# First products of two expert layers by seven block products instead of eight, in a fused attention and two-expert kernel

## The chip, the cores and the metric

One core of a Trainium2 chip runs the whole program. The metric is device time in microseconds. Times are read from one profiled execution (its span runs from the first to the last instruction on the engines) and from three runs without a profile. TensorE (PE) multiplies, and its weight loads (PEld) are listed apart; VectorE (DVE), ScalarE (ACT) and GpSimd (Pool) do the rest, and SyncE (SP) issues the transfers.

## What is computed

Attention with hashed buckets on 16 heads (2 x 8) of 768 tokens, then a gated expert, then a second expert, on 1536 tokens of 512 features:

```
def _moe_ref(x, w_gate, w_val, w_out, rms_g) -> np.ndarray:
    rms = np.sqrt(np.mean(x * x, axis=-1, keepdims=True) + 1e-06)
    xn = x / rms * rms_g
    g = xn @ w_gate
    silu = g * (1.0 / (1.0 + np.exp(-g)))
    val = xn @ w_val
    return (silu * val @ w_out).astype(np.float32)
...
def _moe2_ref(x, w_in, w_out) -> np.ndarray:
    h = x @ w_in
    alpha = 1.0
    g = np.where(h > 0.0, h, alpha * (np.exp(np.minimum(h, 0.0)) - 1.0))
    return (g @ w_out).astype(np.float32)
```

The first expert has 1536 hidden features (12 tiles of 128), the second 2048 (16 tiles). The weights come in as 64-bit floats.

## The kernel before, in words

Every number that enters a matmul is kept as a high and a low word (two reduced-precision floats that add up to it), and each product is made in three passes (`PASS`, L948 and on): high by high, high by low, low by high. ACT makes the high word by a copy, DVE or Pool the low word by a subtraction.

*Attention* comes first: eight pairs of heads, with scores (`ps_s`, L557), transposes (`ps_p`, L602) and weighted sums (`ps_v`, L649). Its output, scaled and split, is `xn`: for each of two batches of 768 tokens, four depth tiles of 128 features.

*Expert one* goes through its 12 hidden tiles in groups of 3, 3, 2, 2, 2 (`SIZES`), and each group through blocks of tokens: four of 384 in the first group, three of 512 after (`BW`; the middle block straddles the two batches, so Pool copies it together, `mid`, L1003). `hidden` makes, for one tile and one block, the gate and value products (`proj_mm`, L993: 4 depth tiles x 3 passes each), then silu on ACT (L1036), the product of both on DVE (L1042), and the high and low words of the result (ACT L1057, DVE L1061) into one of four `pt` buffers. `reduce1` (L1079) multiplies a group's tiles by `w_out` into PSUM (`ps_y`, L1096) and adds the result to the running sum `ya` on DVE (L1108). After the last group `ya` is split into `y` (L1113, L1117).

*Expert two* goes the same way in groups of 3, 3, 3, 3, 2, 2 with 512 tokens a block; its nonlinearity takes exp on ACT and two DVE operations (L1045, L1051). `reduce_cols` (L1137) writes `ps_o` (L1151), with tokens on the rows, and DVE adds it to `oa` (L1163).

*Weights* of the next group are loaded by SP and turned from 64-bit to 32-bit floats: ACT takes the magnitude of the upper half (L891), Pool clamps it (L894), DVE shifts and joins bits in three steps (L900, L907, L914), and then ACT and Pool make high and low words (L936, L940).

PSUM has four single banks (`bank`: `ps_h` and the attention's) and two double ones (`bank2`: `ps_s`, `ps_y`, `ps_o`); each queue runs in the order in which the program issues it. That order is one written list, `ORDER`, of all planned tasks: `Plan.add` collects tasks with their reads and writes, and `Plan.run` issues them as the list says.

## Time and profile before

| | us |
|---|---|
| median of three runs | 808.13 (805.48 to 808.89) |
| the profiled execution's own time | 808.29 |
| its span | 806.5 |
| PE busy in the span | 793.1 |
| DVE busy | 576.0 |
| ACT busy | 414.8 |
| Pool busy | 347.4 |

The granted clock of PE has a mean of 0.998 of full speed (2.4 GHz). The matmuls of neighbouring rows overlap, so a mean duration is longer than the distance from one start to the next; the distance is read from the chain of waits, where rows follow one another.

### The profile page before, as it was taken

How to read it: one execution, taken by the hardware profiler on the slowest of the kernel's cores; microseconds unless marked ns; L12 is line 12 of the kernel's file. 1: busy time of each engine (PE TensorE's matmuls, PEld its weight loads, DVE VectorE, ACT ScalarE, POOL GpSimd, SP SyncE). 2: the span in 40 equal slices, each digit the busy share in tenths (PEclk: the TensorE clock that was granted, in tenths of full speed). 3: DMA queues.
4: the chain of work that ended last, by engine and by line, in shares of the span. 5: the costliest groups of instructions: out<-in, count | busy, mean ns of one | idle time of the engine just before them, and what ended most of it. 6: DMA issues, size and time to landing. Idle time of an engine off the chain costs nothing.

```text
span 806.5 us, 11405 instructions
## 1 busy us (share of the span) xinstructions
PE 793.1 (98%) x4282; PEld 690.9 (86%) x4282; DVE 576.0 (71%) x864; ACT 414.8 (51%) x776; POOL 347.4 (43%) x317
## 2 busy tenths in 40 slices
PE   8999999989999999999999999999999999999998
PEld 6999899878989998888888888888888888888786
DVE  7899999998986835525455567588656686784776
ACT  7999999988985733412222232354433243323230
POOL 5898889987887214212221233221231042221300
PEclk9999999999999999999999999999999999999999
DMA  5537653261021013104002222223203210112004
GB/s 193 183 110 256 227 150 108 98 187 30 1 79 41 1 41 130 53 1 130 3 26 78 79 66 67 77 79 118 78 1 118 60 46 27 52 28 78 0 1 157
DMA packets 28695, 65.64 MB, mean 81 GB/s; under 512 B 3040, under 2 KB 3424, under 8 KB 28640
## 3 DMA queue, kind: packets, MB, share of 16 engines
q1 hardware_dynamic: 28640, 64.91, 25.3%
q8 instruction: 34, 0.56, 0.3%
q14 instruction: 21, 0.17, 0.1%
HBM read 56.25 MB, written 3.15 MB: 74 GB/s over the span
## 4 chain that ended last, share of the span: by engine, by line
PE 82%; DVE 11%; ACT 2%; issue 2%; POOL 1%; DMA 1%; ACTq 0%; SPq 0%; DVEq 0%; POOLq 0%
PE ps_h L993 38%; PE ps_o L1151 16%; PE ps_y L1096 12%; PE ps_v L649 5%; PE ps_p L602 5%; PE ps_s L557 4%; DVE nm L564 3%; DVE pt L614 2%; DVE wf L907 1%; DVE h L1061 1%; ACT p L574 1%; ACT pt L610 1%; DVE wf L914 1%; PE ps_c L484 1%; DVE wf L900 1%
## 5 line engine op out<-in xcount | busy, mean ns | idle before, releaser
L940 POOL TENSOR_TENSOR wlo<-wf,whi 128x768 fp32r<-128x768 f32 (+1 forms) x54 | 90.7, 1687 | 187.8 <-ACT whi L936 171.7
L993 PE MATMUL ps_h<-xn,whi 128*128 128x512 f32 (+1 forms) x480 | 138.3, 369 | 0.0
L894 POOL TENSOR_SCALAR wf<-wf 128x768 f32<-128x768 f32 (+1 forms) x54 | 45.5, 848 | 198.7 <-ACT wf L891 198.2
L1151 PE MATMUL ps_o<-whi,h 128*128 128x512 f32 (+1 forms) x388 | 118.9, 387 | 0.5 <-DVE h L1061 0.4
L993 PE MATMUL ps_h<-y,whi 128*128 128x512 f32 x384 | 118.2, 389 | 0.0
L1057 ACT CAST h<-hf 128x512 fp32r<-128x512 f32 (+1 forms) x87 | 52.0, 605 | 125.1 <-DVE hf L1042 66.0
L993 PEld LDWEIGHTS ps_h<-xn,whi 128*128 128x128 f32 x480 | 88.4, 188 | 11.7
L649 PE MATMUL ps_v<-pt,vv 128*128 128x256 f32 x576 | 94.9, 293 | 2.2 <-DVE ot L667 2.2
L1036 ACT ACTIVATE sg<-ps_h 128x512 f32<-128x512 f32 (+1 forms) x87 | 49.9, 580 | 91.4 <-PE ps_h L993 59.5
L1061 DVE TENSOR_TENSOR h<-hf,h 128x512 fp32r<-128x512 f32 (+1 forms) x87 | 68.7, 806 | 34.9 <-ACT h L1057 34.7
L564 DVE TENSOR_REDUCE nm<-ps_s 128x1 f32<-128x768 f32 x96 | 90.6, 946 | 3.0 <-PE ps_s L557 2.2
L574 ACT ACTIVATE p<-ps_s,nm 128x768 f32<-128x768 f32 x96 | 87.4, 911 | 8.1 <-DVE nm L564 6.8
L1096 PE MATMUL ps_y<-h,whi 128*128 128x512 f32 (+1 forms) x312 | 91.2, 373 | 0.3 <-DVE h L1061 0.3
L557 PE MATMUL ps_s<-tk,tq 128*128 128x384 f32 x384 | 87.9, 350 | 1.5 <-ACT p L574 1.0
L993 PE MATMUL ps_h<-xn,wlo 128*128 128x512 f32 (+1 forms) x240 | 88.2, 367 | 0.0
L614 DVE TENSOR_TENSOR pt<-ps_p,pt 128x512 fp32r<-128x512 f32 x120 | 80.6, 682 | 10.5 <-ACT pt L610 9.7
L1151 PEld LDWEIGHTS ps_o<-whi,h 128*128 128x128 f32 x388 | 72.6, 188 | 16.2 <-DVE h L1061 0.8
L993 PEld LDWEIGHTS ps_h<-y,whi 128*128 128x128 f32 x384 | 72.1, 188 | 14.9
L649 PEld LDWEIGHTS ps_v<-pt,vv 128*128 128x128 f32 x576 | 80.0, 190 | 5.6 <-DVE ot L667 2.5
L602 PE MATMUL ps_p<-ident,p 128*128 128x128 f32 x576 | 82.5, 276 | 1.9 <-DVE pt L614 0.8
L1151 PE MATMUL ps_o<-wlo,h 128*128 128x512 f32 (+1 forms) x194 | 75.1, 387 | 0.0
L993 PE MATMUL ps_h<-y,wlo 128*128 128x512 f32 x192 | 74.7, 389 | 0.0
(102 smaller groups left out, 1419.7 us busy)
## 6 DMA issues: line engine op xcount, KB each, us to landing
wraw<-in_moe_w_out_dram SPq DMA_DIRECT2D x12, 768.0 KB, 4.6
qk<-in_heads_dram SPq DMA_DIRECT2D x16, 384.0 KB, 5.2
wraw<-in_moe_w_in_dram SPq DMA_DIRECT2D x8, 768.0 KB, 4.5
qq<-in_heads_dram SPq DMA_DIRECT2D x14, 384.0 KB, 5.3
kk<-in_heads_dram SPq DMA_DIRECT2D x14, 384.0 KB, 5.6
wraw<-in_moe_w_out_dram SPq DMA_DIRECT2D x10, 512.0 KB, 4.1
tq<-tq SPq DMA_DIRECT2D x21, 192.0 KB, 3.3
vn<-in_v_dram SPq DMA_DIRECT2D x8, 384.0 KB, 5.8
```

What stands on the lines that cost most here:

```text
L557: nc.tensor.matmul(st[B_][:, hf, 0:HS], lhsT=tq[:, x, c * 128:(c + 1) * 128], rhs=tk[:, x, hf * HS:(hf + 1) * HS], start=(x == 0), stop=(x ...
L564: nc.vector.tensor_reduce(out=st["nm", u, cc], in_=st[B_][:, :, 0:HS], axis=AX.XY, op=ALU.max, negate=True,)
L574: nc.scalar.activation(out=halves(st["p", u][:, cc]), in_=st.pop(B_)[:, :, 0:HS], func=AF.Exp, bias=st["nm", u, cc], scale=1.0, accum_out= ...
L602: nc.tensor.transpose(out=st[B_][:, o:o + 128], in_=p[:, cc, (2 * n + kt) * 128:(2 * n + kt + 1) * 128], identity=ident,)
L614: nc.vector.tensor_tensor(out=pt[:, 1], in0=st.pop(B_), in1=f(pt[:, 0]), op=ALU.subtract)
L649: nc.tensor.matmul(st[B_][:, 0:256], lhsT=st["vv", j][:, a, 2 * n + kt, :], rhs=pt[:, x, kt * 256:(kt + 1) * 256], start=(n == seq[0] and ...
L940: nc.gpsimd.tensor_tensor(out=l, in0=s["w"], in1=f(h), op=ALU.subtract)
L993: nc.tensor.matmul(ps[:, o:o + ln], lhsT=w[wp][:, kk, ft * 128:(ft + 1) * 128], rhs=t[xp][:, s:s + ln], start=(kk == 0 and n == 0), stop=( ...
L1057: nc.scalar.copy(out=st["h", g, blk, ft][:, 0, 0:bw], in_=s["hf"])
L1061: nc.vector.tensor_tensor(out=h[:, 1, 0:bw], in0=s["hf"], in1=f(h[:, 0, 0:bw]), op=ALU.subtract)
L1096: nc.tensor.matmul(s["ps"][:, 0:bw], lhsT=wo[wp][:, ft, m * 128:(m + 1) * 128], rhs=h[:, xp, 0:bw], start=(ft == 0 and i == 0), stop=(ft = ...
L1151: nc.tensor.matmul(s["ps"], lhsT=h[:, xp, t * 128:(t + 1) * 128], rhs=wo[wp][:, ft, ds], start=(ft == 0 and i == 0), stop=(ft == n - 1 and ...
```

## The change

The first products of both experts are made of blocks. The two batches (768 tokens each) are the two block rows, the two halves of the depth (256 features each) the inner blocks, and two hidden tiles the two block columns. A pair of block columns then has eight block products; the new code makes seven, of sums of blocks, and adds them up (Strassen's scheme). In expert one a pair is the gate and the value of one hidden tile, and nine of twelve tiles go this way; in expert two a pair is two hidden tiles, and seven pairs (14 of 16 tiles) do. The first three tiles of expert one and the first two of expert two (`G2`) are still made directly, in blocks of 384 tokens. In the new source the lines of the old operations have moved: L993 is L1065, L1096 is L1158, L1108 is L1170, L1151 is L1218, L1163 is L1231.

- `pair(q, j)`: the seven products for one pair and one half (384 tokens) of each batch, 6 matmuls each (L1518), in three PSUM banks. Bank `ps_wA` collects products 1, 6, 7 and 4 one after the other and is read after each: copies by ACT (L1536), then additions by DVE (L1539); `ps_wC` collects 5 and 3, `ps_wE` holds 2. The two (expert one, L1586, L1596) or four (expert two, L1558, L1569) hidden tiles come out as high and low words as before. The second DVE step of the old nonlinearity of expert two becomes a Relu on ACT (L1555).
- `pair_weights`: loads and converts one pair's weights at a time, in pieces of 512 columns (L1372 to L1391), makes four sums of weight blocks on Pool (L1442) and seven split operands (ACT L1452, Pool L1456).
- `spread_x` and `spread_t`: form and split the four sums of token blocks of each expert, for both depth tiles (DVE and Pool, L1314, L1327; L1258, L1269). Two of the four go to Pool (`TPOOL`).
- `reduce1` takes one hidden tile a time in the nine pairs, so a group has three matmuls, and DVE adds to `ya` nine times more, not four; in `reduce_cols` a group is always two tiles.
- The copies for the middle block go, and `ORDER` is a new list for the whole program, attention included. In attention the operations are the same, but for two Pool operations of the first pair that are cut in halves.

```diff
-SIZES = ((3, 3, 2, 2, 2), (3, 3, 3, 3, 2, 2))
+SIZES = ((3,), (2,))
...
     def width(g):
-        return BW[min(g, 1)]
+        return HS
...
+    def h1(g, blk, ft):
+        return ("h", g, blk, ft) if g == 0 else ("wh", g[1], blk % 2, blk // 2)
     def reduce1(g, blk, m, prio):
-        li, f0, n, first, last = groups[g]
+        n, first, last = (groups[0][2], True, False) if g == 0 else (1, False, g == ("w", (0, NPW[0] - 1)))
...
+    def last2(g):
+        return g == ("w", (1, NPW[1] - 1))
+    def h2(g, blk, ft):
+        return ("h", g, blk, ft) if g == G2 else ("wh", g[1], blk % 2, 2 * ft + blk // 2)
...
+        n, first, last = 2, g == G2, last2(g)
...
+        for k in range(2):
+            step(5, k, (0, k), (1, k), (0, k), pos)
+            step(7, k, (1, k), (1, 2 + k), (1, k), pos)
+            step(6, k, (1, 2 + k), (1, 2 + k), (0, k), pos + 1)
+            step(4, k, (0, 2 + k), (0, 2 + k), (1, 2 + k), pos + 1)
+            split(5, k, (0, k), pos + 1)
+            split(7, k, (1, k), pos + 1)
+            split(6, k, (1, 2 + k), pos + 2)
+            split(4, k, (0, 2 + k), pos + 2)
...
+        for k in range(2):
...
+            step("Pool", n7, c, a, SUB, [*xk(k), *xk(2 + k)], [N7], prio)
+            step("Pool", a, a, bh, SUB, nk(k, 0), xk(k), prio)
+            step("Pool", a, a, bl, SUB, nk(k, 1), xk(k), prio)
+            step("DVE", c, c, a, SUB, xk(k), xk(2 + k), prio)
+            step("DVE", n4, dh, c, SUB, [*nk(2 + k, 0), *xk(2 + k)], [N4], prio)
+            step("DVE", n4, n4, dl, ADD, nk(2 + k, 1), [N4], prio)
+            split(7, k, n7, [N7], prio)
+            split(5, k, a, xk(k), prio)
+            split(6, k, c, xk(2 + k), prio)
+            split(4, k, n4, [N4], prio)
...
+        def comb(to, a, b, op):
+            def go():
+                nc.gpsimd.tensor_tensor(out=blk(*to), in0=blk(*a), in1=blk(*b), op=op)
+            plan.add(
+                "Pool", pool(256), go, [(F_[w[0]], w[1]) for w in (a, b) if w != to], [(F_[to[0]], to[1])], prio
+            )
...
+        op(1, (0, 0))
+        comb((0, 2), (0, 0), (0, 1), ALU.subtract)
+        comb((0, 1), (0, 1), (1, 1), ALU.add)
+        op(5, (0, 1))
+        op(2, (1, 0))
+        comb((1, 2), (0, 1), (0, 0), ALU.subtract)
+        op(6, (1, 2))
+        op(7, (0, 2))
+        comb((1, 0), (1, 0), (1, 2), ALU.subtract)
+        op(4, (1, 1))
+        op(3, (1, 0))
...
+    def pair(q, j, prio):
...
+        cs = slice(j * HS, (j + 1) * HS)
+        A_, C_, E_ = (("bank", x, q, j) for x in ("wA", "wC", "wE"))
+        XS = [("wt", q, j, 0), ("wt", q, j, 1), ("hf", "w", q, j, 2), ("hf", "w", q, j, 3)]
...
+        def prod(n, bk, start):
+            if start:
+                s[bk] = bank(bk)[:, 0:HS]
+            w = st["W", q, n]
+            for k in range(2):
+                x = st[xop(q[0], n, k)]
+                for i, (wp, xp) in enumerate(PASS):
+                    nc.tensor.matmul(
+                        s[bk], lhsT=w[:, wp, k], rhs=x[:, xp, cs],
+                        start=start and k == 0 and i == 0, stop=k == 1 and i == 2, skip_group_check=not start,
+                    )
...
+        def tmpx(i):
+            if i not in s:
+                tag = "wt" if i < 2 else "hf"
+                s[i] = tmp.tile([128, HS], F32, tag=tag, name=tag)
+            return s[i]
...
+        def copy(i, bk="ps_wA"):
+            nc.scalar.copy(out=tmpx(i), in_=s[bk])
+        def add(to, i, bk):
+            nc.vector.tensor_tensor(out=tmpx(to), in0=s[bk], in1=tmpx(i), op=ALU.add)
...
+            def a1():
+                e["g"] = tmp.tile([128, HS], F32, tag="sg", name="sg")
+                nc.scalar.activation(out=e["g"], in_=val(), func=AF.Exp)
+            def a2():
+                nc.scalar.activation(out=e["g"], in_=e["g"], func=AF.Relu, bias=ones[:, 0:1], scale=-1.0)
+            def d3():
+                nc.vector.scalar_tensor_tensor(
+                    out=tmpx(xi), in0=val(), scalar=0.0, in1=e["g"], op0=ALU.max, op1=ALU.subtract
+                )
...
+            plan.add("ACT", act(HS), a1, [key], [G_], prio, tab="exp")
+            plan.add("ACT", act(HS, 1), a2, [], [G_], prio)
+            plan.add("DVE", dve(HS), d3, [key, G_] if key == A_ else [G_], [K_], prio)
+            plan.add("ACT", act(HS) + 0.043, hi, [K_], [(H_, 0)], prio)
...
+        def silu(i):
+            nc.scalar.activation(out=tmpx(i), in_=tmpx(i), func=AF.Silu)
...
+            def mul():
+                nc.vector.tensor_tensor(
+                    out=tmpx(xi), in0=tmpx(xi) if o else s["ps_wA"], in1=tmpx(o), op=ALU.mult
+                )
...
+            plan.add("DVE", dve(HS), mul, [XS[o], *key], [XS[xi]], prio)
+            plan.add("ACT", act(HS) + 0.043, hi, [XS[xi]], [(H_, 0)], prio)
+            plan.add("Pool" if gp else "DVE", pool(HS) if gp else dve(HS), lo, [XS[xi], (H_, 0)], [(H_, 1)], prio)
+        P(1, A_, "ps_wA", True, [("wgo", q, j)])
+        plan.add("ACT", act(HS), lambda: copy(0), [A_], [XS[0]], prio)
+        P(5, C_, "ps_wC", True)
+        plan.add("ACT", act(HS), lambda: copy(2, "ps_wC"), [C_], [XS[2]], prio)
+        P(6, A_, "ps_wA", False)
+        plan.add("ACT", act(HS), lambda: copy(1), [A_], [XS[1]], prio)
+        P(2, E_, "ps_wE", True)
+        plan.add("DVE", dve(HS), lambda: add(0, 0, "ps_wE"), [E_], [XS[0]], prio)
+        if q[0]:
+            out(0, 0, XS[0], 0)
+        else:
+            plan.add("ACT", act(HS), lambda: silu(0), [], [XS[0]], prio, tab="silu")
+        P(7, A_, "ps_wA", False)
+        plan.add("DVE", dve(HS), lambda: add(2, 2, "ps_wA"), [A_], [XS[2]], prio)
+        if q[0]:
+            out(3, 1, XS[2], 2)
+        P(4, A_, "ps_wA", False)
+        if q[0]:
+            out(2, 1, A_, 3)
+        else:
+            gated(0, [A_])
+        P(3, C_, "ps_wC", False)
+        plan.add("DVE", dve(HS), lambda: add(1, 1, "ps_wC"), [C_], [XS[1]], prio)
+        if q[0]:
+            out(1, 0, XS[1], 1)
+        else:
+            plan.add("ACT", act(HS), lambda: silu(1), [], [XS[1]], prio, tab="silu")
+            gated(1, [])
...
+    spread_x(pos)
+    pair_weights((0, 0), pos, [("go", NPAIR - 1)])
+    late = [(0, prev)]
+    for li in range(2):
+        reduce_, nr = (reduce1, KD) if li == 0 else (reduce2, 3)
+        if li:
+            for blk in (0, 2, 1, 3):
+                for pg, pb in late:
+                    for m in range(KD if pg != G2 else 3):
+                        (reduce1 if pg != G2 else reduce2)(pg, pb, m, pos)
+                if blk == 0:
+                    spread_t()
+                for ft in range(groups[G2][2]):
+                    hidden(G2, blk, ft, pos)
+                    hid += 1
+                    pos += 1.0
+                late = [(G2, blk)]
...
+        for n in range(NPW[li]):
+            for j in range(2):
+                pair((li, n), j, pos)
+                if j == 0:
+                    if n + 1 < NPW[li]:
+                        pair_weights((li, n + 1), pos + 1, [("wgo", (li, n), 0)])
+                    elif li == 0:
+                        for todo in wtasks(G2):
+                            weights(*todo, pos + 0.5, [("wgo", (li, n), 0)])
+                        pair_weights((1, 0), pos + 4, [("wgo", (li, n), 0)])
+                pos += 2.0
+                for pg, pb in late:
+                    for m in range(KD if li == 0 else 3):
+                        reduce_(pg, pb, m, pos)
                 pos += 1.0
...
+                late = [(("w", (li, n)), j), (("w", (li, n)), 2 + j)]
+    for pg, pb in late:
+        for m in range(3):
+            reduce2(pg, pb, m, pos)
```

What the list does to the queues is seen at two places, each before and after. First PE, expert one, before: the end of one first product and the reductions of a two-tile group behind it (`ps_h` first product, `mid` and `xn` its tokens, `ps_y` reduction; the numbers tell buffers apart).

```order
L993 MATMUL ps_h_5639<-mid_3763,whi_5405 128x512
L993 MATMUL ps_h_5639<-mid_3764,whi_5405 128x512
L993 MATMUL ps_h_5639<-mid_3763,wlo_5406 128x512
L1096 MATMUL ps_y_5654<-h_5635,whi_5534 128x512 x2
L1096 MATMUL ps_y_5654<-h_5635,wlo_5535 128x512
L1096 MATMUL ps_y_5654<-h_5637,whi_5534 128x512 x2
L1096 MATMUL ps_y_5654<-h_5637,wlo_5535 128x512
L1096 MATMUL ps_y_5666<-h_5635,whi_5534 128x512 x2
```

Each reduction is six matmuls of 512 columns for one feature tile, two hidden tiles by three passes. In the new list the same place of the program, the sixth pair or so of expert one (`T` are sums of token blocks, `W` the pair's split weights):

```order
L1158 MATMUL ps_y_4732<-h_4651,whi_4580 128x384 x3
L1518 MATMUL ps_wA_4739<-xn_3283,W_4628 128x384 x3
L1518 MATMUL ps_wA_4739<-xn_3229,W_4628 128x384 x3
L1158 MATMUL ps_y_4756<-h_4651,whi_4580 128x384 x3
L1158 MATMUL ps_y_4762<-h_4608,whi_4580 128x384 x3
L1518 MATMUL ps_wE_4772<-xn_3306,W_4697 128x384 x3
L1518 MATMUL ps_wE_4772<-xn_3267,W_4697 128x384 x3
L1158 MATMUL ps_y_4780<-h_4651,whi_4580 128x384 x3
L1158 MATMUL ps_y_4793<-h_4651,whi_4580 128x384 x3
L1518 MATMUL ps_wA_4739<-T_4195,W_4713 128x384 x3
L1518 MATMUL ps_wA_4739<-T_4151,W_4713 128x384 x3
L1158 MATMUL ps_y_4806<-h_4767,whi_4580 128x384 x3
```

A reduction is now one row of three, reductions and block products alternate, and two products that add into the same bank (`ps_wA_4739`) stand eight rows apart.

Then DVE in the same stage, before (`wf` is a weight conversion, `hf` the product of gate and value, `h` the low word):

```order
L1108 TENSOR_TENSOR ya<-ps_y,ya 128x512
L900 TENSOR_SCALAR wf<-wf 128x512
L907 SCALAR_TENSOR_TENSOR wf<-wraw,wf 128x512
L914 SCALAR_TENSOR_TENSOR wf<-wraw,wf 128x512
L1061 TENSOR_TENSOR h<-hf,h 128x512 x2
L1108 TENSOR_TENSOR ya<-ps_y,ya 128x512 x2
```

The reduction sums are 512 wide and stand among conversions and low words. In the new list the same engine has:

```order
L1596 TENSOR_TENSOR h<-hf,h 128x384
L1539 TENSOR_TENSOR wt<-ps_wC,wt 128x384
L1170 TENSOR_TENSOR ya<-ps_y,ya 128x384 x2
L1539 TENSOR_TENSOR hf<-ps_wA,hf 128x384
L1170 TENSOR_TENSOR ya<-ps_y,ya 128x384
L1539 TENSOR_TENSOR wt<-ps_wE,wt 128x384
L1170 TENSOR_TENSOR ya<-ps_y,ya 128x384
L1586 TENSOR_TENSOR hf<-hf,wt 128x384
L1170 TENSOR_TENSOR ya<-ps_y,ya 128x384 x2
L1596 TENSOR_TENSOR h<-hf,h 128x384
L1586 TENSOR_TENSOR hf<-ps_wA,wt 128x384
L1170 TENSOR_TENSOR ya<-ps_y,ya 128x384 x2
```

The low words are still there (the conversions stand in other rows); between the reduction sums `ya` now stand the block additions out of `ps_wA`, `ps_wC` and `ps_wE`, and the reduction sums are 384 wide and three times as many.

## Rows read from the trace of the kernel before

**Rows 1.** Busy shares of the whole span (the page).

```profile
PE 793.1 (98%) x4282; PEld 690.9 (86%) x4282; DVE 576.0 (71%) x864; ACT 414.8 (51%) x776; POOL 347.4 (43%) x317
```

**Rows 2.** Busy time of each engine by stage (us from the span's start: length, busy us and instructions of PE, PEld, DVE, ACT, Pool, clock, DMA).

```profile
40.00:175.00 135.00, 133.52 (x1004) 124.53 (x1003) 129.02 (x197) 126.95 (x258) 120.89 (x111) 1.00 0.53 166
235.00:339.00 104.00, 103.68 (x589) 99.32 (x589) 60.28 (x93) 51.56 (x94) 41.68 (x44) 1.00 0.20 61
339.00:534.00 195.00, 195.00 (x862) 161.49 (x861) 105.75 (x158) 57.19 (x99) 49.33 (x44) 1.00 0.20 63
535.00:789.00 254.00, 253.47 (x1118) 209.22 (x1116) 179.57 (x268) 92.58 (x154) 54.02 (x41) 1.00 0.15 48
```

**Rows 3.** Costliest groups, shapes apart, PE: line, names, shape, count, busy us, mean ns.

```profile
L993 PE MATMUL ps_h<-y,whi 128*128 128x512 f32 x384 | 118.2, 389 | 0.0
L993 PE MATMUL ps_h<-xn,whi 128*128 128x384 f32 x192 | 49.5, 338 | 0.0
```

**Rows 4.** The chain of waits in order of time: start us, length us, what.

```profile
263.37 2.08 PE ps_h L993 x12
542.11 2.72 PE ps_h L993 x12
544.83 1.36 PE ps_y L1096 x6
```

**Rows 5.** Who PE waited for from 290 to 806 us: total, times, longest.

```profile
PE ps_o L1151 <- DVE h L1061: 0.4, 1, 0.4
PE ps_y L1096 <- DVE h L1061: 0.3, 1, 0.3
```

**Rows 6.** Costliest groups, shapes apart, DVE over the whole span.

```profile
L1163 DVE TENSOR_TENSOR oa<-ps_o,oa 128x512 f32<-128x512 f32 x59 | 40.1, 687 | 43.4 <-PE ps_o L1151 42.9
L907 DVE SCALAR_TENSOR_TENSOR wf<-wraw,wf 128x512 int32<-128x512 int32 x26 | 19.2, 741 | 0.5
L914 DVE SCALAR_TENSOR_TENSOR wf<-wraw,wf 128x512 int32<-128x512 int32 x26 | 19.4, 748 | 0.4
L900 DVE TENSOR_SCALAR wf<-wf 128x512 int32<-128x512 int32 x26 | 14.9, 576 | 4.0 <-POOL wf L894 4.0
L1061 DVE TENSOR_TENSOR h<-hf,h 128x384 fp32r<-128x384 f32 x12 | 9.0, 763 | 10.7 <-ACT h L1057 10.7
L1042 DVE TENSOR_TENSOR hf<-ps_h,sg 128x384 f32<-128x384 f32 x12 | 6.7, 557 | 13.6 <-PE ps_h L993 7.0 <-ACT sg L1036 6.5
```

**Rows 7.** Durations of one line's instructions: ns min/median/max, first and last start.

```profile
L1061 DVE TENSOR_TENSOR h<-hf,h x87: 548/685/2185, 258.8 to 795.5; 128x512 fp32r<-128x512 f32 x75, 128x384 fp32r<-128x384 f32 x12
L914 DVE SCALAR_TENSOR_TENSOR wf<-wraw,wf x54: 679/948/3716, 97.6 to 775.7; 128x768 int32<-128x768 int32 x28, 128x512 int32<-128x512 int32 x26
```

**Rows 8.** Costliest groups, DVE from 40 to 175 us, first and last of ten.

```profile
L564 DVE TENSOR_REDUCE nm<-ps_s 128x1 f32<-128x768 f32 x58 | 54.7, 945 | 1.0 <-PE ps_s L557 0.5
L690 DVE RECIPROCAL r<-r 128x12 f32<-128x12 f32 x5 | 1.1, 219 | 0.6 <-POOL r L685 0.5
```

**Rows 9.** The chain in the attention stage, and PE's groups from 40 to 175 us.

```profile
24.26 0.44 PE ps_p L602 x4
24.70 0.48 PE ps_v L649 x4
25.18 0.70 PE ps_s L557 x4
...
L649 PE MATMUL ps_v<-pt,vv 128*128 128x256 f32 x341 | 56.3, 291 | 0.0
L557 PE MATMUL ps_s<-tk,tq 128*128 128x384 f32 x229 | 52.5, 349 | 0.4 <-issue 0.3
L602 PE MATMUL ps_p<-ident,p 128*128 128x128 f32 x344 | 49.3, 275 | 0.9 <-DVE pt L614 0.5
```

**Rows 10.** Costliest groups, Pool.

```profile
L626 POOL TENSOR_TENSOR pt<-pf,pt 128x512 fp32r<-128x512 f32 x24 | 31.4, 1309 | 1.0
L738 POOL TENSOR_TENSOR sq<-sq 128x768 f32<-128x768 f32 x5 | 9.2, 1836 | 0.2
```

More of the change, by code (lines that the diff above doesn't have):

```diff
@@ L865, in weights @@
             view = src[:, f0 * 128:(f0 + n) * 128].rearrange("(k p) f -> p k f", p=128)
-        view = wpart(view, g, m, part)
+        if g == G2:
+            view = view[:, part:part + 1] if nm == "wo" else view[:, 2 * part:2 * part + 2]
+        else:
+            view = wpart(view, g, m, part)
         shape = list(view.shape)
@@ L997, in proj_mm @@
             )
[L999 to L1015 removed]
     def wkeys(g, m):
+        if g == G2:
+            return [(("h3", x, g, m, p), p) for x in ("whi", "wlo") for p in range(2)]
         return [(("slot", x, g, m), p) for x in ("whi", "wlo") for p in range(2)]
@@ L1168, in store @@
             )
-        hk = [(("pt", "h", g, blk, ft), p) for ft in range(n) for p in range(2)]
-        plan.add(
-            "PE", 3 * n * mm(wd), lambda: [pe(ft) for ft in range(n)], hk + wkeys(g, 1), [B_], prio
-        )
+        hk = [(("pt", *h2(g, blk, ft)), p) for ft in range(n) for p in range(2)]
+        wk = wkeys(g, 1) if g == G2 else [(("slot", x, g), p) for x in ("who", "wlow") for p in range(2)]
+        plan.add("PE", 3 * n * mm(wd), lambda: [pe(ft) for ft in range(n)], hk + wk, [B_], prio)
         if first:
```

352 lines of the change are left out of this document (266 added, 86 removed), and 333 rows, old and new, of the table ORDER.

## The prediction

> **What bounds the kernel now.** I read the busy shares first [rows 1]: TensorE (PE) is busy 793.1 of 806.5 us, VectorE (DVE) 576.0. Then the stages [rows 2]. From 339 to 789 us, where both experts run, PE is busy without a gap (195.0 of 195.0 us and 253.5 of 254.0), while DVE fills 54% and 71% and GpSimd (Pool) 25% and 21%. A busy PE may still be slow, since its rows overlap, so the next view is the chain of waits, which gives the pace from start to start [rows 4]: twelve products of 512 columns take 2.72 us (0.2267 us each), twelve of 384 take 2.08 us (0.1733 each). The mean durations beside them [rows 3] are longer (389 and 338 ns) because a product drains while the next streams; they are not used for the sum. Last, who PE waited for in the experts [rows 5]: 0.7 us in all. So before, PE streams at its pace through both experts, and a product removed there is time removed, as long as the others keep up.
>
> **The change, part by part.**
>
> *Products removed.* In first products, the old code has 648 of 512 columns for expert one outside its first group (9 of 12 tiles, gate and value, 3 blocks, 4 depths, 3 passes) and 576 for expert two; the reduction of those 9 tiles has 324 ([rows 3] show the form; the passes with the low word are half as many again). That is 1548 x 0.2267 = 350.9 us. The new code has, per pair and half of the tokens, 7 block products of 6 matmuls of 384 columns: 16 pairs x 2 x 42 = 1344, then 96 for the two direct tiles of expert two, and 432 in the reduction: 1872 x 0.1733 = 324.5 us. **Saving on PE: 26.4 us.** One eighth of the columns goes; a little comes back because 384 columns carry the same fixed cost (0.0133 us over the column time at 2.4 GHz, by the two rows) more often. The second products of expert two stay at 128x512.
>
> The Trainium skill (TensorE: Matmul & The Clock Gate, Back-to-back issue gap) gives the isolated spacing as N/2.4 + 2.5 ns, so 215.8 and 162.5 ns; by it the saving would be an estimated 29.8 us. The trace's pace is 11 and 11 ns slower, and the trace decides.
>
> *DVE, expert one.* One pair now costs DVE, for both halves: 6 block additions out of PSUM, 2 multiplications out of PSUM, 16 reduction additions (one tile each instead of two or three, so three times as many): 24 x 0.557 = 13.4 us; 2 multiplications and 4 low words with both operands in SBUF at 0.763: 4.6; three weight conversions of 512 at 0.576 + 0.741 + 0.748 = 2.07: 6.2 [rows 6]. Sum **24.2 us**, against 84 + 48 matmuls on PE, 132 x 0.1733 = **22.9 us**. These durations overlap where DVE is pressed. The attention stage shows by how much: from 40 to 175 us ten groups of DVE work have durations of 141.1 us in 135 us ([rows 8] are the first and the last). At that density, 1.045, a pair needs 23.2 us of DVE: a hair more than PE.
>
> *DVE, expert two.* Per pair 8 x 0.557 + 14 x 0.763 + 12 x 0.687 + 4 x 2.07 = 31.7 us, 30.3 at the same density, against 84 x 0.1733 + 72 x 0.2267 = 30.9 us of PE. So DVE goes from half-idle to level with PE in both experts. The old expert-two minimum/subtract (48 on DVE) moves to ACT, which has room [rows 1].
>
> *What this costs PE.* PE waits more often now: each reduction group of three matmuls (0.52 us) reuses one of two banks and waits for the DVE addition two groups back, where the old groups took 1.36 us or more. Behind a waiting group stands the next block product in PE's queue, for that ACT's copy out of PSUM, and for that the next accumulation into the same bank, so a late addition moves all of it. No row shows this state in the experts. Lower bound: nothing, as now [rows 5]. Nearest row: attention, where DVE is busy 129.0 of 135 us [rows 2] and PE's matmuls at their pace (341 at 0.48/4, 229 at 0.70/4, 344 at 0.44/4, and some 11 us for 90 others) come to 130 us [rows 9], so 3.8% is lost. Upper bound: the last rival below. I take 3.8% for the nine pairs of expert one (206 us): **+7.9**, and a third of it for expert two (249 us), where groups are 1.36 us long again and DVE is under PE: **+3.2**.
>
> *Sums of tokens.* Before each expert, token sums are formed and split: 10 and then 8 operations of 768 columns on DVE, and as many on Pool at 1.84 us [rows 10]. For expert one they lie beside the last of the first group (about 75 us of PE work from its start at 235 us); Pool was busy 41.7 of 104 us there [rows 2], so 18 us fit; the 16 copies for the old middle block go away. If that cover fails, the first products with token sums wait, up to Pool's 18 us. For expert two, 15 us of Pool lie beside the direct tiles, 96 x 0.1733 + 72 x 0.2267 = 33 us of PE. Hidden if the last sums of expert one arrive in time; between 0 and 6 us (one DVE queue of ten operations late), I take **+2**.
>
> *Weight sums.* Per pair Pool does 4 sums and 7 low words of 256 columns, about 0.78 us each by the slope of the two Pool rows [rows 10], one low word of 512 and three clamps: about 12 us in 22.9. Off the path, but Pool's share doubles; see the last rival. Weight loads rise from 54 to 83 on SP's queue, with the same bytes, where DMA moved 48 to 63 GB/s [rows 2]; they are asked for a pair (22.9 us) ahead: 0, and if one lands late, the pair's first product waits that long. Attention keeps its work, in a new order; up to 5 us either way, taken as 0.
>
> Sum on the profiled execution's 808.3 us (span 806.5; the median of three runs is 808.1, so no correction): 808.3 - 26.4 + 7.9 + 3.2 + 2.0 = **795.0 us**.
>
> **The rivals.**
>
> 1. *PE keeps streaming.* The order on PE puts some five groups (3 us or more) between two products that add into one bank, so DVE's lag is absorbed: 808.3 - 26.4 = 782, to 785 with the seam. For it: 0.7 us of waits now [rows 5]. Against: that was with DVE half idle.
>
> 2. *Most is given back.* The full attention loss of 3.8% in both experts and 6 us at the seam: 26.4 - 7.9 - 9.5 - 6 leaves 3 us, 805; a result from 804 to 812 counts here, within 0.5% of now, about what a measurement of this kernel can tell from no change.
>
> 3. *DVE becomes the bound, slower.* A DVE operation with both operands in SBUF is held up when Pool works: the low word takes 0.548 us at best and 2.185 at worst, and conversion steps reach 3.716 [rows 7]; the 384-column low word averages 0.763, 0.21 above its best, with Pool at 40%. There are 15 such operations per pair of expert one, 26 of expert two, and Pool's share there doubles. If each conversion step takes 0.1 us more and the waits leave DVE no overlap, a pair costs 25.4 and 32.7 us of DVE, 2.5 and 1.8 over PE: 9 x 2.5 + 7 x 1.8 = 35 us, so 808.3 - 26.4 + 35 = **817**. It decides from 1.65 us of stall per pair (26.4 / 16). Against: in attention Pool is busy 120.9 of 135 us [rows 2] and PE still loses only 3.8%.
> The Trainium skill (SBUF — State Buffer, Who interferes with whom) says that such a DVE operation contends with a GpSimd operation that reads SBUF, and that the later one blocks until the other ends; by that rule the new Pool sums land on the new DVE low words. The spread of [rows 7] agrees.
>
> **How the numbers follow.** Forecast, 785 to 804: 0.54, because the nearest row has every engine pressed harder than the experts will be. Rival 1: 0.18. Rival 2: 0.14. Rival 3: 0.14. Faster by over 0.5% (under 804): 0.72; within: 0.14; slower: 0.14. Range 781 to 812: its low end is the sum without any stall, its top leaves out rival 3 and little else.
>
> **What would show it.** In the new profile: 12 matmuls of 384 columns still in 2.08 us; PE's busy time down by some 15 to 26 us; DVE's up from 576 to some 720 or 730 (the pairs alone are 9 x 24.2 + 7 x 31.7 = 440 us by durations, where the two stages had 285); PE's waits in the experts mostly on DVE, on the reduction sums and the block additions, each well under a microsecond and 11 to 15 us in sum, more of them in expert one; Pool near half busy there. Forecast wrong if PE's waits there stay under 3 us (rival 1), if they pass 26 us with DVE at 95% or more (rival 3), if PE's granted clock falls from 1.00, or if the time changed in attention, before 235 us.

## The result, and the profile after

The changed kernel takes **799.37 us** (median of four runs, 798.86 to 800.93) against 807.67 for the kernel before beside it: a ratio of **0.9903, 95% interval 0.9877 to 0.9929**. The forecast was 795.0 (781 to 812). It is faster, by some 8 us of the 13 that were expected. The sum was nearly right; the places were not. The profiled execution, the longest of the four, took 800.93 us; its span is 799.0.

The page of the changed kernel: the busy time of each engine, then tenths of busy time in 40 slices of 20 us.

```profile
PE 778.2 (97%) x4606; PEld 730.4 (91%) x4606; DVE 697.5 (87%) x1145; ACT 526.6 (66%) x1098; POOL 484.1 (61%) x489
...
PE   9999899999999999999999999986999999999998
...
PEclk9999999999999999999999999988899999999999
```

Beside [rows 1], PE's busy time is 14.9 us lower and DVE's 121.5 us higher. New is a hole in the 27th and 28th slice, from 519 to 559 us: PE's busy share falls to 0.8 and 0.6, and its granted clock to 0.8, one slice longer. This is where expert one ends and expert two begins. Four stretches show it more sharply (columns as in [rows 2]):

```profile
320.00:480.00 160.00, 160.00 (x921) 159.19 (x920) 146.47 (x269) 78.75 (x180) 87.74 (x105) 1.00 0.23 70
480.00:520.00 40.00, 39.30 (x220) 37.49 (x219) 39.54 (x73) 20.34 (x44) 20.96 (x22) 1.00 0.39 125
520.00:580.00 60.00, 51.04 (x229) 46.81 (x229) 49.83 (x77) 33.24 (x66) 32.13 (x24) 0.86 0.05 14
580.00:780.00 200.00, 199.77 (x996) 179.32 (x995) 172.22 (x289) 129.75 (x277) 90.21 (x103) 1.00 0.19 60
```

In the pairs of expert one (first line) and of expert two (last), PE is busy without a gap although DVE now fills 92% and 86% where [rows 2] had 54% and 71%. Between them PE stands idle for 9.0 of 60 us, at a mean clock of 0.86. The seven largest waits of PE from 320 us to the end (total, times, longest) all lie there but the last:

```profile
PE ps_h L1065 <- DVE hf L1108: 3.1, 1, 3.1
PE ps_o L1218 <- DVE ya L1170: 1.9, 1, 1.9
PE ps_o L1218 <- DVE h L1118: 1.7, 1, 1.7
PE ps_y L1158 <- ACT h L1592: 0.9, 1, 0.9
PE ps_y L1158 <- DVE h L1596: 0.7, 1, 0.7
PE ps_y L1158 <- DVE ya L1170: 0.6, 1, 0.6
PE ps_wA L1518 <- ACT wt L1536: 0.5, 1, 0.5
```

Where [rows 5] had 0.7 us, there are now 9.4. The pace itself is unchanged ([rows 4] had 2.08 for twelve); the chain of waits has:

```profile
576.08 2.08 PE ps_wA L1518 x12
```

One more reading gives the ledger. For every matmul of 512 or 384 columns from 240 us on I took the distance from its start to the next start, less 0.2267 or 0.1733 us, and added these up: 2.8 us before, **24.7** after. By stretch the 24.7 are 0.8 (to 320 us), 3.0 (320 to 520), **17.7** (520 to 580) and 3.2 (580 to the end). The first product of expert one also starts earlier. Before, and then after (start, duration):

```profile
235.57 0.51 PE L993 MATMUL ps_h<-xn,whi 128*128 128x384 f32 x2
```

```profile
232.61 0.52 PE L1065 MATMUL ps_h<-xn,whi 128*128 128x384 f32 x2
```

So from span to span, 806.5 to 799.0: -26.4 for the products, +21.9 of new waiting (24.7 - 2.8), -3.0 from attention. The sum is the measured -7.5.

The last of these terms rests on one profile of each kernel. The profile of before has a wait in attention that ends at 181.1 us and that the new one has not (total, times, longest):

```profile
PE ps_v L649 <- DVE ot L667: 2.2, 1, 2.2
```

Right behind it, from 182.0 us on, the granted clock is 0.50 for 3.4 us. Of the 29 executions of the kernel before beside the experiments, the 16 with a mean clock of 1.000 average 806.5 us and the 13 others 808.5. So some 2 of the 3.0 us may belong to that one execution and not to the new order; this was not tested.

### The profile page after: what moved, and what is told of

Its sections match the earlier page's. It is cut to its first block, busy times and chain, and to the rows that moved or that the text cites. A ratio compares the mean times of both kernels' runs of the same rounds, so it can differ in the third digit from the quotient of the medians.

```text
span 799.0 us, 13085 instructions
## 1 busy us (share of the span) xinstructions
PE 778.2 (97%) x4606; PEld 730.4 (91%) x4606; DVE 697.5 (87%) x1145; ACT 526.6 (66%) x1098; POOL 484.1 (61%) x489
## 4 chain that ended last, share of the span: by engine, by line
PE 83%; DVE 7%; ACT 5%; issue 2%; DMA 1%; POOL 1%; SPq 0%; ACTq 0%; POOLq 0%; DVEq 0%
PE ps_o L1218 16%; PE ps_wA L1518 16%; PE ps_y L1158 12%; PE ps_h L1065 8%; PE ps_wC L1518 8%; PE ps_s L620 6%; PE ps_v L712 6%; PE ps_p L665 6%; PE ps_wE L1518 4%; ACT p L637 2%; ACT pt L673 1%; DVE nm L627 1%; DVE pt L677 1%; DMA kk<-in_heads_dram 1%; DVE y L1179 1%
## 5 line engine op out<-in xcount | busy, mean ns | idle before, releaser
L1456 POOL TENSOR_TENSOR W<-wf,W 128x256 fp32r<-128x256 f32 x112 | 96.0, 871 | 57.9 <-ACT W L1452 54.5
L1218 PE MATMUL ps_o<-whi,h 128*128 128x512 f32 (+1 forms) x388 | 120.0, 390 | 3.6 <-DVE ya L1170 1.9
L1158 PE MATMUL ps_y<-h,whi 128*128 128x384 f32 x528 | 115.9, 339 | 2.4 <-ACT h L1592 0.9
L1518 PE MATMUL ps_wA<-T,W 128*128 128x384 f32 x576 | 115.8, 335 | 0.5 <-ACT wt L1536 0.5
L1518 PEld LDWEIGHTS ps_wA<-T,W 128*128 128x128 f32 x576 | 101.6, 188 | 3.0 <-ACT wt L1536 1.2
L1158 PEld LDWEIGHTS ps_y<-h,whi 128*128 128x128 f32 x528 | 94.0, 190 | 4.8 <-DVE ya L1170 2.0
L1218 PEld LDWEIGHTS ps_o<-whi,h 128*128 128x128 f32 x388 | 72.1, 189 | 16.7 <-issue 2.2
L1170 DVE TENSOR_TENSOR ya<-ps_y,ya 128x384 f32<-128x384 f32 x144 | 76.0, 550 | 10.4 <-PE ps_y L1158 10.1
L1442 POOL TENSOR_TENSOR wf<-wf 128x256 f32<-128x256 f32 x64 | 54.6, 853 | 43.5 <-DVE wf L1391 39.6
L1218 PE MATMUL ps_o<-wlo,h 128*128 128x512 f32 (+1 forms) x194 | 76.1, 392 | 0.0
L673 ACT CAST pt<-ps_p 128x512 fp32r<-128x512 f32 x120 | 69.3, 588 | 10.3 <-PE ps_p L665 7.5
L665 PEld LDWEIGHTS ps_p<-ident,p 128*128 128x128 f32 x576 | 66.6, 141 | 10.3 <-DVE pt L677 3.0
L1231 DVE TENSOR_TENSOR oa<-ps_o,oa 128x512 f32<-128x512 f32 (+1 forms) x85 | 57.2, 680 | 20.1 <-PE ps_o L1218 19.8
L620 PEld LDWEIGHTS ps_s<-tk,tq 128*128 128x128 f32 x384 | 63.0, 189 | 5.1 <-ACT p L637 3.0
```

The source lines that it names most:

```text
L620: nc.tensor.matmul(st[B_][:, hf, 0:HS], lhsT=tq[:, x, c * 128:(c + 1) * 128], rhs=tk[:, x, hf * HS:(hf + 1) * HS], start=(x == 0), stop=(x ...
L665: nc.tensor.transpose(out=st[B_][:, o:o + 128], in_=p[:, cc, (2 * n + kt) * 128:(2 * n + kt + 1) * 128], identity=ident,)
L673: nc.scalar.copy(out=st[T_][:, 0], in_=st[B_])
L1158: nc.tensor.matmul(s["ps"][:, 0:bw], lhsT=wo[wp][:, ft, m * 128:(m + 1) * 128], rhs=h[:, xp, 0:bw], start=(ft == 0 and i == 0), stop=(ft = ...
L1170: nc.vector.tensor_tensor(out=ya, in0=s["ps"][:, 0:bw], in1=ya, op=ALU.add)
L1218: nc.tensor.matmul(s["ps"], lhsT=h[:, xp, t * 128:(t + 1) * 128], rhs=(wo[wp][ft][:, 0] if g == G2 else wo[wp][:, ft])[:, ds], start=(ft = ...
```

## The experiments

Twelve kernels, all made from the changed one. Medians in us; the ratio is to the kernel before, run beside them (807 to 808).

| run | what | median | ratio, 95% interval |
|---|---|---|---|
| the change | | 799.37 | 0.9903 [0.9877, 0.9929] |
| eight | one product twice in each pair and half | 829.65 | 1.0274 [1.0239, 1.0309] |
| lo2 | low words of expert one's pairs twice | 821.81 | 1.0177 [1.0143, 1.0211] |
| lo2_two | low words of expert two's pairs twice | 823.39 | 1.0199 [1.0170, 1.0229] |
| fill | 52 idle matmuls at PE's waits | 798.84 | 0.9890 [0.9868, 0.9913] |
| notsum | token sums of expert two left out | 791.93 | 0.9796 [0.9757, 0.9836] |
| notsum_noylo | and low words of y left out | 788.64 | 0.9756 [0.9734, 0.9778] |
| notsum_noylo_noconv | and DVE steps of 8 conversions left out | 786.32 | 0.9732 [0.9710, 0.9753] |
| tsum_dve | token sums of expert two all on DVE | 797.89 | 0.9885 [0.9858, 0.9912] |
| tsum_pool | the same all on Pool | 803.43 | 0.9950 [0.9932, 0.9968] |
| ylo_pool | low words of y on Pool | 801.12 | 0.9923 [0.9898, 0.9948] |
| reorder | two moves on DVE's queue | 800.89 | 0.9919 [0.9893, 0.9945] |
| best | tsum_dve with fill | 798.92 | 0.9886 [0.9866, 0.9905] |

The profiles of these thirteen, whose attention is the same, have expert one's first product start anywhere from 230.6 to 233.6 us. So a difference below 3 us between two single spans says little, and stretches are compared by what PE does in them.

### Does PE set the pace in the pairs, and has DVE room?

**eight:**

```
-        P(2, E_, "ps_wE", True)
+        P(2, E_, "ps_wE", True, twice=True)
...
-                "PE", 6 * mm(HS), lambda: prod(n, bk, start),
+                "PE", 6 * mm(HS), lambda: [prod(n, bk, start) for _ in range(1 + twice)],
```

> An eighth product's worth of matmuls is put back: in every pair and half the product into ps_wE is made twice into the same bank (the second overwrites the first), 16 x 2 x 6 = 192 more matmuls of 384 columns and nothing else. Theory S (in the pairs PE still sets the pace; what was lost of the saving was lost between the experts, from 500 to 580 us): 192 x 0.1733 = 33.3 us more, 832 to 833. Rival D (in the pairs DVE sets the pace with PE, so a product is worth little there): under 20 us more, below 820.

Measured: 30.3 us more, of the 33.3 that the matmuls take. PE sets the pace in the pairs, and a product taken out there is worth what the pace says. (The excess over the pace, added up as above, is 20.6 us there where the change has 24.7; these 4.1 us cover the missing three.) With the longer pairs DVE gets air, 133.2 us of 160 where it had 146.5:

```profile
320.00:480.00 160.00, 159.94 (x923) 159.62 (x922) 133.18 (x246) 72.25 (x165) 77.11 (x93) 1.00 0.19 62
```

**lo2:**

```
-                (nc.gpsimd if gp else nc.vector).tensor_tensor(
-                    out=h[:, 1, 0:HS], in0=tmpx(xi), in1=f(h[:, 0, 0:HS]), op=ALU.subtract
-                )
+                for _ in range(2):
+                    nc.vector.tensor_tensor(
+                        out=h[:, 1, 0:HS], in0=tmpx(xi), in1=f(h[:, 0, 0:HS]), op=ALU.subtract
+                    )
```

> In the nine pairs of expert one every low word is formed twice on DVE, the same value: 36 more operations of 0.64 us by their mean there, 23 us of DVE, 2.6 us a pair. From 320 to 480 us DVE is busy about 9.1 of every 10 us, so a pair of 22.9 us leaves some 2 us free. Theory S (DVE has that little room and no more): the first 2 us of each pair are hidden, 0 to 8 us more, 799 to 807. Rival D (DVE already sets the pace there): the whole 23 us, about 822.

Measured: 22.4 us more, nearly all of the 23. Here theory S said 0 to 8 and fell. In the same stretch PE now loses 8.1 of 160 us, and the waits that opened (310 to 560 us) are on the reduction sums:

```profile
320.00:480.00 160.00, 151.94 (x839) 144.02 (x837) 150.99 (x269) 71.49 (x162) 80.41 (x92) 1.00 0.20 63
```

```profile
PE ps_y L1158 <- DVE ya L1170: 10.8, 17, 1.8
```

DVE does not go above 94% even so. The 8% that it stood idle in the changed kernel were no room; they are its own waits, above all for PE's reductions (8.7 of the 13.5 us, in 13 waits for `ps_y`). Together with eight: in expert one the two engines are level. More work on either lengthens the run by nearly all of it. Whether the added operations cost this by their sum, or by their place ahead of reduction sums in DVE's queue, was not separated.

**lo2_two** does the same in expert two (the same edit in `out`).

> The same test in expert two: in its seven pairs every low word is formed twice on DVE, 56 more operations of about 0.69 us, 38 us of DVE, 5.5 us a pair. From 580 to 780 us DVE is busy 172 of 200 us, so a pair of 30.9 us leaves 4.3 us free by the busy share. If idle time of DVE is room: 5.5 - 4.3 = 1.2 us a pair appear, 8 to 12 us more, 808 to 811. If it is not (as in expert one, where 22.4 of 23 us appeared although DVE had stood idle for 8% of the time): 25 us or more, above 824.

Measured: 24.0 us more of some 38. It lies between the two, near the second: some 14 us of DVE's work found room, not the 30 that its idle share promised. PE's waits from 570 us on are on ACT's copy out of the bank, which stands behind DVE in the chain, and on the sums of expert two:

```profile
PE ps_wA L1518 <- ACT wt L1536: 8.5, 10, 2.1
PE ps_o L1218 <- DVE oa L1231: 4.0, 4, 1.7
```

### Is it the clock between the experts?

The stretches of half clock and one between them, after (columns as above):

```profile
520.00:524.00 4.00, 2.26 (x10) 1.36 (x9) 4.00 (x10) 2.95 (x7) 0.00 (x0) 0.98 0.64 196
524.50:530.50 6.00, 6.00 (x19) 6.00 (x20) 5.15 (x9) 2.57 (x4) 1.86 (x2) 0.50 0.00 0
531.00:539.00 8.00, 8.00 (x48) 8.00 (x47) 7.63 (x16) 3.51 (x8) 3.56 (x3) 1.00 0.02 4
544.50:547.50 3.00, 2.83 (x8) 2.64 (x9) 2.45 (x5) 2.09 (x5) 2.66 (x2) 0.50 0.00 0
558.00:564.50 6.50, 5.54 (x17) 5.54 (x18) 6.11 (x12) 1.99 (x4) 0.00 (x0) 0.50 0.00 0
```

PE idles for 1.7 of 4 us; right after, the granted clock is 0.50, the lower of the two levels (1.2 GHz), while PE works all the time, and then 1.00 again. In the three stretches at 0.50 PE is busy for 14.4 us, which is 7.2 us of work at the full clock.

**fill** (`idle` runs behind five tasks of the list, the last ones of PE ahead of a wait; the numbers name the tasks and count the matmuls):

```
+FILL = {2637: 3, 2675: 12, 2707: 10, 2751: 9, 2777: 18}
...
         for i in ORDER:
             self.tasks[i][2]()
+            for _ in range(FILL.get(i, 0)):
+                self.idle()
...
+    def idle():
+        nc.tensor.matmul(
+            st["last"][:, 1, 0:HS], lhsT=wsel[:, 0, 0], rhs=bitt[0], start=True, stop=True
+        )
```

> PE gets 52 more matmuls of 384 columns (52 x 0.1733 = 9.0 us) at the five places between the experts where it waited, 3, 12, 10, 9 and 18 of them, into the unused half of a double bank; nobody reads them. Theory C (after each wait the granted clock stood at 0.5 for 3.4 to 6.8 us, and PE, which was working again by then, set the pace): in the trace PE worked 6.1, 3.0 and 5.9 us at half clock, which loses half of that, 7.5 us; with the clock at 1.00 throughout the time falls by 4 to 8 us, to 791 to 795. Rival W (the waits themselves are the loss; while PE ran slowly DVE, ACT and Pool caught up, so a faster PE would only wait longer): the clock's dip goes or not, and the time stays within 2 us of 799, or rises by the matmuls that fall beside a wait.

```profile
520.00:580.00 60.00, 56.62 (x293) 52.52 (x293) 52.00 (x80) 35.28 (x71) 32.35 (x25) 0.97 0.06 18
```

Two of the three dips are gone (0.97 for the stretch), and the time is 798.84, 0.5 us below: the intervals lie on one another. Rival W holds, with this reservation: a filler that ran past the end of a wait cost its own 0.17 us, so a small gain may be hidden in it. PE's 17.7 us of excess became 6.3 and 9.0 us of fillers, 15.3, so these two profiles differ by 2.4 us there, of the 7.2 that the half clock could have cost. For the rest, a PE at full clock came sooner to the next thing that was not finished; its waits between the experts are again on DVE. What has to be explained is DVE.

### What holds PE up between the experts?

Three kernels, each leaving out more. **notsum**: the products with token sums read y tiles (their high and low words) in place of `T`, and the tasks of `spread_t` do nothing:

```
-            eng.tensor_tensor(out=o, in0=a, in1=c, op=ALU.subtract)
+            pass
...
-                x = st[xop(q[0], n, k)]
+                x = st[("y2", *{4: (0, 2 + k), 5: (0, k), 6: (1, 2 + k), 7: (1, k)}[n]) if q[0] and n > 3 else xop(q[0], n, k)]
```

> Leaves out the token sums of expert two: its products 4 to 7 read plain y tiles in place of the sums, so that 8 operations on DVE, 8 on Pool and 8 copies on ACT go, all of them from about 535 to 575 us; PE's matmuls are the same. Theory T (the sums and their port conflicts hold up DVE's low words and the nonlinearity of the direct tiles, and so PE at 539 to 559 us): the waits from 539 us on, 7.0 us of the 18.9, and the dips of the clock behind them, 4.4 us, go, 788 to 791. Rival R (the loss is the tail of expert one, whose last reduction sums and splits of y are late on a DVE that is full from 480 to 525 us): the wait at 520 to 525 us and the dip behind it stay, and later waits only move; 796 to 800.

**notsum_noylo**: and in `reduce1` the step `lo` that makes y's low word (L1179) does nothing, and the products read the high word twice.

> Leaves out the token sums of expert two, as the run without them (791.9), and the 16 low words of y as well (11.8 us on DVE from 513 to 548 us); the products read the high word in their place, so PE's matmuls are the same. Theory A (DVE's work in the tail of expert one is what PE waits for at 520 to 545 us): 4 to 6 us less than 791.9, 786 to 788. Rival H (it is the chain reduction, sum, high word, product of the last hidden tile, with nothing else for PE to do): 790 to 792, PE still waits at 520 to 525 us.

**notsum_noylo_noconv**: and the three DVE steps of a conversion do nothing for the direct tiles and the first pair of expert two; Pool's clamp is set to 0.03 there, so that the numbers stay small.

```
+            if g == G2:
+                c3 = c4 = c5 = lambda: None
```

> Leaves out, beside those, the three DVE steps of the 8 weight conversions of expert two's direct tiles and first pair (24 operations, some 17 us of DVE between 495 and 565 us; the weights are then other numbers). If DVE's load there is all of the loss: PE's excess over its pace from 500 to 580 us, 18.9 us in the changed kernel and 11.9 without token sums, falls under 3 us, 780 to 783. If the last chain of expert one is what stays: 4 to 8 us of excess are left, and the time is within 2 us of the run before it in this list.

The stretch from 520 to 580 us of the three, in this order:

```profile
520.00:580.00 60.00, 54.51 (x265) 49.29 (x264) 42.20 (x77) 33.94 (x73) 16.50 (x20) 0.94 0.15 49
```

```profile
520.00:580.00 60.00, 56.16 (x287) 50.76 (x287) 37.66 (x69) 38.01 (x80) 18.71 (x21) 1.00 0.15 53
```

```profile
520.00:580.00 60.00, 57.76 (x296) 52.41 (x297) 32.37 (x58) 37.69 (x80) 20.46 (x25) 1.00 0.16 52
```

The time falls from 799.4 to 791.9, 788.6 and 786.3; PE's idle time in the stretch from 9.0 to 5.5, 3.8 and 2.2 us; and the excess over the pace there from 17.7 to 10.8, 5.8 and 3.9. So the **token sums** are the largest part (some 7 us, theory T), and the conversions are 2.

What y's **low words** cost is less certain, because the median of notsum stands between two pairs. Two of its four executions took 789.4 and 789.5 us, with a mean clock of 1.000. The other two, one of them the profiled one, took 794.3 and 794.5, with 0.995 and 0.996; the profile has the clock at 0.50 twice, for 3.4 us each. notsum_noylo has 1.000 in all four. Without y's low words the time is 0.8 us less than that of the first pair (as rival H has it) and some 6 less than that of the second (as theory A has it). By the pairs the token sums are worth 10 or 5 us. Here, unlike in fill, a lower clock goes with 5 us; whether the clock makes them or the waits ahead of it was not tested.

DVE's load there was not "all of the loss": some 4 us stay, with the wait for the nonlinearity of a direct tile on top:

```profile
PE ps_h L1067 <- DVE hf L1110: 1.4, 1, 1.4
```

That rest was not taken apart.

### DVE's amount of work, or its company?

DVE's work in the token sums is only 8 operations, 7.6 us at their best. In the changed kernel the groups of DVE from 500 to 580 us include (busy us, mean ns):

```profile
L1179 DVE TENSOR_TENSOR y<-ya,y 128x384 fp32r<-128x384 f32 x16 | 11.8, 754 | 0.0
L1118 DVE TENSOR_TENSOR h<-hf,h 128x384 fp32r<-128x384 f32 x8 | 6.4, 808 | 0.0
L1258 DVE TENSOR_TENSOR ya<-ya 128x768 f32<-128x768 f32 x4 | 5.9, 1497 | 0.0
```

and single operations on Pool and then on DVE (start, duration):

```profile
548.62 2.16 POOL L1269 TENSOR_TENSOR T<-ya,T 128x768 fp32r<-128x768 f32 x1
...
554.39 1.96 POOL L1269 TENSOR_TENSOR T<-ya,T 128x768 fp32r<-128x768 f32 x1
```

```profile
549.00 4.01 DVE L1258 TENSOR_TENSOR ya<-ya 128x768 f32<-128x768 f32 x2
554.30 0.36 DVE L1102 TENSOR_SCALAR sg<-sg 128x384 f32<-128x384 f32 x1 [1.29 <-ACT sg L1093]
554.58 2.19 DVE L1118 TENSOR_TENSOR h<-hf,h 128x384 fp32r<-128x384 f32 x1
...
561.09 0.95 DVE L1258 TENSOR_TENSOR ya<-ya 128x768 f32<-128x768 f32 x1
```

Two sums take 4.01 us beside Pool's low word and its work on weights behind it; the same sum takes 0.95 once Pool is quiet. A low word of a direct tile started at 554.58, 0.19 us after Pool's; it ended at 556.77, 0.42 us after Pool's did. PE's longest wait, 3.1 us up to 558.96, stands right behind these in DVE's queue.

The Trainium skill (SBUF — State Buffer, Who interferes with whom) says that a DVE operation with both inputs in SBUF contends with a GpSimd operation that reads SBUF, that the one that issues later blocks, and that one with at most one SBUF input does not contend, outside what the page calls the 2-port perf modes. The trace agrees for the low word, and for the reduction sum, which has one operand in PSUM and took 541 to 560 ns in all its 144 instances. But having a single SBUF input was no protection for the step L1102: 0.36 us by its median, it took 1.29 us at 539.39, beside a sum on Pool (538.32 to 540.47). In which mode it ran no run here shows.

The delay also passes through ACT. Its queue has the copy of a sum's high word (L1265) ahead of the exponential of the next direct tile (L1093):

```profile
553.04 0.84 ACT L1265 CAST T<-ya 128x768 fp32r<-128x768 f32 x1 [2.91 <-DVE ya L1258]
553.78 0.48 ACT L1093 ACTIVATE sg<-ps_h 128x384 f32<-128x384 f32 x1
```

PE had finished that tile's product at 551.3 us. ACT waited until 553.04 for the slow sum, and DVE then stood idle for 1.29 us, until 554.30, for the exponential behind it. The chain of waits that ends in PE's longest wait runs through these steps and then through the low word above.

**tsum_dve** and **tsum_pool** (`TPOOL2` takes the place of `TPOOL` in `spread_t`; in tsum_pool it is `(4, 5, 6, 7)`):

```
+TPOOL2 = ()
```

> The token sums of expert two that Pool made (4 sums and 4 low words of 768 columns, 1.8 to 2.2 us each, 16 us in all, from 535 to 556 us) are made on DVE instead, 0.95 us each. Theory P (Pool's sums hold up the DVE operations beside them; a sum on DVE took 2.0 us there against 0.95 a few microseconds later, a low word 2.2 against 0.55): DVE gets back some 6 us and takes 7.6 more, and Pool's long operations are no longer waited for: within 2 us of the change, 797 to 801. Theory L (what counts is how much DVE has to do between the experts): 7.6 us more on the queue that PE waits for, 803 to 807.

> The token sums of expert two that DVE made (8 operations of 768 columns, some 10 us) are made on Pool instead, 8 more of about 2 us there. Theory L (DVE's load between the experts): most of what leaving the sums out brought (7.4 us) comes, 793 to 796. Theory P (conflicts with Pool): Pool works 16 us longer beside DVE, and the last sums come later: no gain or a loss, 798 to 805, with PE waiting for Pool's T at the first products of expert two.

With all sums on DVE, 7.6 us more for the engine that PE waits for, the time is 797.89, not 803 to 807: no slower. With all on Pool, which relieves DVE, it is 803.43, slower than the change (the intervals don't meet). Both times lie where theory P had them, and outside theory L's. The last clause of P did not come: PE did not wait for Pool's `T`. The low word of the direct tiles shows what Pool's company costs a single operation. First tsum_dve, then tsum_pool (groups of DVE, 520 to 580 and 515 to 580 us); the same eight operations stand at 808 ns in the change:

```profile
L1119 DVE TENSOR_TENSOR h<-hf,h 128x384 fp32r<-128x384 f32 x8 | 5.3, 671 | 0.0
```

```profile
L1119 DVE TENSOR_TENSOR h<-hf,h 128x384 fp32r<-128x384 f32 x8 | 9.7, 1236 | 3.6 <-ACT h L1115 3.6
```

In tsum_dve PE's excess over its pace is 20.4 us, 4.3 less than in the change; the medians differ by 1.5. In tsum_pool it is 26.0, only 1.3 more, in a profiled execution (800.60 us) that was the shortest of seven; so this profile shows a part of the 4 us between the medians. In it PE's three longest waits for DVE are no longer than in the change. New is one for ACT:

```profile
PE ps_h L1066 <- DVE hf L1109: 3.0, 1, 3.0
PE ps_o L1219 <- DVE ya L1171: 1.9, 1, 1.9
PE ps_o L1219 <- ACT oa L1228: 1.8, 2, 1.2
PE ps_o L1219 <- DVE h L1119: 1.7, 1, 1.7
```

DVE is not short of time there: it stands idle 5.9 us for ACT's exponentials, once for 3.7 us, up to 550.66. ACT had waited for Pool's sum until 549.40, with that exponential behind the sum's copy. So Pool has two effects, the hold on DVE's operations and sums that come late into ACT's queue. How the 4 us divide between them was not tested.

**ylo_pool** (the 16 low words of y from `nc.vector` to `nc.gpsimd`):

> The 16 low words of y (384 columns; 11.8 us on DVE from 513 to 548 us) are made on Pool, which was idle for 4.9 us before 524 and 8.5 us before 535 us; about 1 us each there. Theory A (the tail of expert one is held up by a DVE that has the reduction sums, the low words of y and the conversions at once): the waits of PE at 520 to 525 us and part of those at 540 to 545 us go, 3 to 6 us less, 793 to 796. Rival B (the low words now come late from a slower engine and the first products of expert two wait for them): 799 to 806, with waits of PE for y on Pool at 526 us.

Measured 801.12: no gain; if anything slower, though the intervals overlap. The words took 1135 ns each on Pool, and the low words of the direct tiles went from 808 to 870 ns on DVE. Neither theory had the mechanism: PE did not wait for y on Pool; its wait for the direct tile's low word grew from 1.7 to 3.7 us. The low word that it waited for took 2.17 us and ended 0.4 us after a pair of sums on Pool, as theory P would have it. But DVE also stood idle once, for 3.6 us, for a low word of y on Pool, which is the lateness of rival B at another engine. What each cost was not separated.

```profile
PE ps_o L1220 <- DVE h L1118: 3.7, 1, 3.7
```

**reorder** (in the list: two conversion steps behind expert one's last low word; two token sums and a low word of a sum behind the nonlinearity of the direct tile):

> Two moves on DVE's queue, nothing added: two conversion steps of expert two's first pair go behind the low words that PE waits for at 520 to 525 us, and the two sums and one low word of token sums (2.0, 2.0 and 1.5 us) that stand ahead of the direct tile's nonlinearity go behind it (PE waited 3.1 us for that one, at 555.5 us). If a late place on DVE's queue is what PE waits for: 1.1 and 3.1 us come back, 795 to 797. If DVE's sum of work in the stretch is what counts: no change, 799, the wait only moves to the first products with token sums.

Measured 800.89, no gain. The waits moved, as the second reading has it: new ones of 2.0 us on a reduction sum and 2.2 us on a block addition took the place of what the 3.1 us wait lost (1.4 is left of it). The line numbers are lower by 194, since the list stands on fewer lines.

```profile
PE ps_y L964 <- DVE ya L976: 2.3, 2, 2.0
PE ps_o L1024 <- DVE ya L976: 2.2, 1, 2.2
PE ps_h L871 <- DVE wt L1345: 2.2, 1, 2.2
PE ps_h L871 <- DVE hf L914: 1.4, 1, 1.4
```

**best:**

> The token sums of expert two all on DVE (797.9 by itself) and the 52 extra matmuls at PE's waits (798.8 by itself), nothing left out. If the two are independent, 1.5 and 0.5 us add to 797.4; if the clock matters only where DVE is not late, more may come, 794 to 796; if both took away the same wait, 798.

Measured 798.92: the two don't add. No kernel that computes everything is faster than the change beyond the intervals; that of tsum_dve, which has the lowest median, covers the change's ratio.

## Why the prediction was right, and where it was not

- **Products removed, -26.4 us: right.** The pace held (2.08 us for twelve of 384), and putting one product back cost 30.3 of 33.3 us. With the earlier start and the new waiting it closes the ledger to 0.1 us.
- **DVE level with PE in expert one: right**, by count (23.2 against 22.9 us a pair) and by lo2, where 22.4 of 23 added us appear.
- **What that costs PE, +7.9 in expert one: wrong.** This is the step "Nearest row: attention ... 3.8% is lost". From 320 to 520 us PE lost 3.0 us, of which 0.8 came before 480. A DVE that is full did not make PE wait, as long as no more is asked of it; why attention loses 3.8% with engines as full was not tried. For expert two the +3.2 were nearly met: 3.2 from 580 us on, of which the kernel before had 1.1.
- **The seam, +2, "between 0 and 6 us": wrong, and the largest miss.** It was 17.7 us between 520 and 580 us. The prediction counted the operations that DVE and Pool have there, each at the price that it has alone, and saw them hidden behind 33 us of direct tiles. It did not count that the last reduction sums, y's low words, the conversions and the token sums all come on DVE at once, in front of the direct tiles that should hide them, nor that Pool's 1.8 to 2.2 us operations hold up DVE's there, nor that ACT's queue has copies of these sums ahead of the direct tiles' exponentials. The token sums of expert one, taken as hidden, were: PE's excess up to 320 us is 0.8.
- **Attention "taken as 0": -3.0 us**, inside the 5 us either way. Most of it may be the one wait and the dip of the clock behind it in the profile of before (see the result), and not the new order.
- The forecast missed the profiled execution (800.9) by 5.9 us: 15.7 too little at the seam, against 5.8 too much in expert one (3.0 there and 0.8 before it, less 1.7 that the kernel before lost too), 1.1 in expert two (3.2 less its 1.1) and 3.0 in attention. Three errors of one sign hid most of a large one of the other; that the time lay so near the forecast is luck.
- **The rivals.** Rival 1 (PE keeps streaming) is what happened inside both experts. Rival 3's mechanism, port conflicts of DVE and Pool, is seen in single operations between them, in one place and not in every pair: low words in the pairs of expert one averaged 0.64 us, less than the 0.763 of [rows 6], though Pool was busy 55% of the time there. Its point of decision, DVE over PE in each pair, was a hair away, as lo2 shows. Its sum has a slip: 0.1 us more for each of 9 and 12 conversion steps makes 25.1 and 32.9 us a pair, so 816 and not 817.
- **The signs.** Named as signs against the forecast were a granted clock below 1.00 and a change in attention. Both came. The first cost 0.5 us by fill's median and 2.4 by the excess in its profile; the second helped. The waits that the forecast named as its own sign did not come: 11 to 15 us of short ones on DVE, more of them in expert one. There were 9.4 us, 6.7 of them in three waits of 1.7 to 3.1 us between the experts. PE's busy time fell by 14.9 us, at the edge of the 15 to 26 named, and DVE's (697.5) stayed under the 720 to 730.
